# Thresholded attention and a gated feed-forward in one kernel: scores of two key tiles in one run, weight sums in another place, new planner costs and ranks

## The chip, the core and the metric

The kernel runs on one core of one Trainium2 chip. The metric is device time in microseconds for one execution. The kernel before was timed three times: 1387.51, 1389.75 and 1391.09 us, median 1389.75. One further execution was profiled; from its first to its last instruction it spans 1385.8 us, and every duration below is from it. Lower is better.

The engines are called by their short names: PE (TensorE, matrix products), DVE (VectorE), ACT (ScalarE), POOL (GpSimd) and SP (the engine that only issues transfers). PEld is PE's loading of weights, which runs beside its products.

## What is computed

```python
# q, k, v: (8, 8, 576, 64) float32; tau = 0.02
scores = (q @ k^T) / sqrt(64)
thresh = max(scores, over keys) - tau
scores = where(scores >= thresh, scores, -1e9)
attn   = softmax(scores)            # with 1e-9 added to the sum
x      = (attn @ v), heads side by side -> (4608, 512)
h      = x @ w_in                   # (512, 2048)
g      = h / (1 + exp(-1.702 * h))
out    = g @ w_out                  # (2048, 512) -> (4608, 512)
```

All products are done in float32. The two weight matrices arrive as float64 and are converted on the chip.

## The kernel before

**Attention, by pairs.** Two heads of one batch element make a pair; there are 32 pairs, four to a batch element. For each pair n the kernel transposes q and k on DVE (`prep`, L390), so that head h lies on partitions 64h to 64h+63. The 576 keys are four tiles of 128 and a tail of 64. For one key tile t and one half c of the 576 queries, `scores` (matmul at L414) issues two matmuls, one for each head, each on 64 of PE's 128 rows, into one PSUM slot of two banks (pool `psA`, three slots). The tail of both heads together is one product over all 128 rows (L407), with a small block-diagonal weight `kd` that POOL copies (`prep_kd`, L395). ACT copies each slot to SBUF (`keep`, L437). DVE takes the maxima (`in_groups` L451, `over_tiles` L457/L462, `over_groups` L471/L472), lowers them by tau and spreads them over partitions by a trip through DRAM (`lower_rows`, `row_out`, `row_in`) for the first pairs, by `lower` (L477/L482) and `spread_max` (L497) later. `sub` (L523/L528) subtracts; ACT masks and exponentiates (L534, L538). `values` (matmul at L552, 64 columns of PE per head) multiplies with v into a psA slot named `pv`. The sums of the exponentials come from PE for pairs 0 to 4 (`sums_by_pe`) and from DVE later (`in_groups` with add, `one_group` L595). `spread_sums` (L604, L606) inverts and spreads them, and `place_x` (L623) writes the scaled result as the transposed x of the feed-forward's blocks. `place_x` gives the `pv` slot back.

PE thus works in three shapes: 64 rows (scores), 64 columns (values and sums), and the whole array (the tail and the feed-forward).

**Feed-forward, by blocks of 256 tokens.** Blocks 0 and 1 are done plainly and together (`first_blocks`: `mm1_0` L678, `mm2` L660 with 512 columns), while w_in and w_out still arrive and are converted (`cv_ex`, `cv_power`, `cv_frac`, `cv_end`). Blocks 2 to 13 (`feed_forward`) take `mm1` (L638), tanh (L647), `gelu` (L650) and then a second product by seven half-size products instead of eight (`second`, `product`, matmul at L825; the results are gathered by `read`, L847). These need sums of quarters of g, made on POOL after every second gelu (`s_sums`, L791 to L793; `s_last`, L804), and sums of quarters of w_out, made once on POOL in eight operations of 128x1024 (`t_sum`, L785). The last four blocks (`two_blocks`) also use seven products for the first matmul (`product1`, L743); they need `w_sum` (L717) and `x_sum` (L726). Accumulators of the feed-forward lie in pool `psM`, two slots of one bank.

**What sets the order.** Nothing is scheduled at run time. Every piece of work is a `task` with an engine, a cost, a rank, the tasks it follows, and the slots it takes and gives back. `run_in_order` plays these through on a clock: whenever an engine is free it starts the ready task of lowest rank for which the slots are there, and emits its instructions at that moment. The result is a fixed order on each engine; on the chip semaphores keep the true dependencies, and each engine works strictly in its order. Feed-forward products on PE have the rank LAST (1000), and so fill what attention leaves. The tables `EARLY`, `LATER` and `CV` shift ranks by the name of a task. `lag` is the time the planner assumes between the end of a task and its use by another engine (0.06 us unless given). From pair `WHOLE` = 6 on, both halves of a key tile are one task that takes two psA slots (`scores_of`); before that each half is a task of its own.

Of the kernel before, what the change touches and what calls it, by code (L numbers as in the profile page):

```python
# [19 lines left out]
P = 128  # L20
# [10 lines left out]
def kernel(  # L31
# [97 lines left out]
    for x in ("raw0", "raw1", "qkT0", "qkT1", "mb"):  # L129
# [6 lines left out]
        "lower_rows": -1.89,  # L136
        "values": 1.63,
        "exps": 1.38,
        "load_qk": -1.72,
        "prep": -1.69,  # L140
        "load_v": 1.46,
        "mask": 1.64,
        "over_groups": -1.9,
        "sub": -1.05,
        "one_group": 0.95,
        "scores": 0.67,
        "spread_sums": 1.4,
        "sums_by_pe": 2.29,
        "in_groups": 0.61,
        "keep": -1.15,  # L150
    }
    LATER = {
        "in_groups": 0.38,
        "mask": -0.74,
    }
    CV = {
        "cv_power": 0.15,
        "cv_frac": 0.13,
    }

    def task(engine, cost, rank, f, *a, after=(), take=(), give=(), lag=0.06):
        if 0 <= rank < LAST:
            rank += CV.get(f.__name__, 0.0) + (EARLY if a[0] < 2 * NPAIR else LATER).get(f.__name__, 0.0)
        tasks.append((engine, cost, rank, f, a, [x for x in after if x is not None],
                      take, give, lag))
        return len(tasks) - 1
# [3 lines left out]
    def run_in_order():  # L170
# [10 lines left out]
        started = 0  # L181
        while events:
# [18 lines left out]
            for engine, queue in ready.items():  # L201
# [12 lines left out]
                heapq.heappush(events, (now + tasks[i][1], 0, i))  # L214
# [187 lines left out]
    def scores(n, t, c):  # L402
        qT, kT = mats[n, 0], mats[n, 1]
        ps = psA.tile([P, 2, 512], FP32, name="ps", tag="ps")
        if t == NKT:
            for i in range(2):
                nc.tensor.matmul(  # L407
                    ps[:, i, 0:SH], lhsT=kd, rhs=qT[:, ts(i, SH)],
                    start=True, stop=True,
                )  # L410
            del mats[n, 0], mats[n, 1]
        else:
            for h in range(2):
                nc.tensor.matmul(  # L414
                    ps[:, h, 0:SH],
                    lhsT=kT[ts(h, D), ts(t, P)], rhs=qT[ts(h, D), ts(c, SH)],
                    start=True, stop=True,
                )
        pss[n, t, c] = ps

    def scores_of(n, t, cs):
        for c in cs:
            scores(n, t, c)
# [474 lines left out]
    FFU = 1.722  # L898
# [3 lines left out]
    for i in range(len(pieces)):  # L902
# [9 lines left out]
        a = task("POOL", 2.4, rank, load_w, i, after=w_loads[-1:], take=place, lag=5.0)  # L912
        w_loads.append(a)
        e = task("DVE", 0.43, rank, cv_ex, i, after=[a])
        m = task("ACT", 0.79, rank, cv_power, i, after=[e])
        a = task("DVE", 1.14, rank, cv_frac, i, after=[e])

        over = [ready_w[y] for y in range(i) if i >= n_in and stage(y) == (i - n_in) // PER_STAGE]
        ready_w.append(task("DVE", 0.7, rank, cv_end, i, after=[a, m] + over, give=place))
# [8 lines left out]
    def first_blocks():  # L928
        xs = list(placed.values())[-NPAIR:]
        for j in range(NFC):  # L930
# [7 lines left out]
            a = task("ACT", 0.6, FIRST, tanh, j, after=ffn[-1:], take=("io",))  # L938
            gelus[j] = task("DVE", 0.69, FIRST, gelu_0, j, after=[a], give=("psM", "io"))
        for i in range(PLAIN * BLK // P):  # L940
# [7 lines left out]
            a = task("ACT", 0.6, FIRST, half, i, after=ffn[-1:], take=("osb",), give=("psM",))  # L948
            task("SP", 0.6, FIRST, store_0, i, after=[a], give=("osb",), lag=2.2)

        for x in range(4):
            for k in range(2):
                after = t_ready[-1:] + (ffn[-1:] if x > 1 else ffn[2 * NFC : 2 * NFC + 1])
                t_ready.append(
                    task("POOL", 3.0, FIRST, t_sum, x, k, after=after + ready_w[n_in:])
                )

    def feed_forward(blk):
# [3 lines left out]
        for j in range(HF):  # L962
            for f in range(2):
# [6 lines left out]
            a = task("ACT", 0.6, FIRST, tanh, j, after=ffn[-1:], take=("io",))  # L970
            gelus[j] = task(
                "DVE", 0.69, FIRST, gelu, j, after=[a, last_mm2.get(j // 4)],
                give=("psM", "io"),
            )
            if j % 2:
                sums.append(task("POOL", 2.5, FIRST, s_sums, j // 2, after=[gelus[j - 1], gelus[j]]))
        second(blk, 0, {j: [gelus[j]] for j in range(HF)}, sums)

    def second(blk, w, ready, sums):
# [4 lines left out]
        for x, p in order:  # L984
            js = ((0, 4), (4, 8), (4, 7), (7, 8))[p]
            after = ffn[-1:] + t_ready
# [15 lines left out]
            if x == P6:  # L1002
                lasts = [task("POOL", 1.6, FIRST, s_last, k, w, after=ffn[-1:]) for k in range(2)]
            if x == P1:
                a = task("ACT", 0.35, FIRST, read, blk, x, after=ffn[-1:], take=("osb", "osb"))
            else:
                a = task(
                    "DVE", 0.84 if x == P5 else 0.42, FIRST, read, blk, x, after=ffn[-1:] + reads,
# [8 lines left out]
    def two_blocks(blk):  # L1017
# [4 lines left out]
        for x in range(4):  # L1022
            if first:
                done_w.append([task("DVE", 0.66, LAST - 1.0, w_sum, x, 0, nc.vector, after=done_w[-1:][0] if done_w else xs)])
            after = (xd[-1:] or xs) + (done_w[x][:1] if first else []) + last_product1
            xd.append(task("DVE", 0.66, LAST - 1.0, x_sum, blk, x, after=after))
        if first:
            for k in range(1, HF // 2):
                for x in range(4):
                    after = xs + done_w[x - 1][-1:] + done_w[x][-1:]  # L1030
                    done_w[x].append(
                        task("POOL", 1.5, FIRST, w_sum, x, k, nc.gpsimd, after=after)
# [3 lines left out]
        for j in range(HF):  # L1036
            reads = [None] * 7
            for x in range(7):
# [6 lines left out]
                if x == P3:  # L1045
                    after += xs
# [5 lines left out]
                if x == P1:  # L1052
                    a = task("ACT", 0.35, FIRST, read1, j, x, after=ffn[-1:], take=("hs",), give=bank)
                else:
                    a = task(
                        "DVE", 0.84 if x == P5 else 0.42, FIRST, read1, j, x,
# [3 lines left out]
            for h in range(2):  # L1060
                a = task("ACT", 0.6, FIRST, tanh1, j, h, after=[reads[P5 if h == 0 else P3]], take=("io",))
                g1[j, h] = task(
                    "DVE", 0.8, FIRST, gelu1, j, h, after=[a, last_mm2.get(j // 4), g1.get((j, 0))],
                    give=("io", "hs") if h else ("io",),
                )
            if j % 2:
                sums.append(task(
                    "POOL", 2.5, FIRST, s_sums, j // 2, after=[g1[j - 1, 0], g1[j, 0]]
# [5 lines left out]
        a = task("DVE", 1.3, FIRST, s_sum1, 0, after=again + ffn[-3:-2])  # L1074
        b = task("DVE", 1.3, FIRST, s_sum1, 1, after=[a] + ffn[-1:])
        c = task("DVE", 1.3, FIRST, s_sum1, 2, after=[b])
# [7 lines left out]
    for n in range(NP):  # L1084
# [4 lines left out]
        slow = 1.2 if n < NPAIR else 1.0  # L1089
# [4 lines left out]
        lq = task("SP", cost, r - 2.0, load_qk, n, 0, q0, after=behind, take=own(n, "raw0"), lag=2.0)  # L1094
        lk = task(
            "SP", cost if n else 0.1, r - 2.0, load_qk, n, 1, q1, after=behind,
            take=own(n, "raw1"), lag=2.0,
        )
        v_tail = f"v_t{n % 2}"
        lv = task("SP", 2.1, r - 1.2, load_v, n, take=("v_m", v_tail), lag=2.0)  # L1100
        pq = task("DVE", 0.77, r, prep, n, 0, after=[lq], take=own(n, "qkT0"), give=own(n, "raw0"))
        pk = task("DVE", 0.77, r, prep, n, 1, after=[lk], take=own(n, "qkT1"), give=own(n, "raw1"))
        pd = task("POOL", 0.5, r, prep_kd, n, after=[pk], take=("kd",))
# [5 lines left out]
        mx = []  # L1109
        for t in range(NKT + 1):  # L1110
            tail = t == NKT
            copies = []
            if tail or n >= WHOLE:


                cs = range(1 if tail else 2)
                a = task(
                    "PE", (1.2 if tail else 1.35) * slow, r, scores_of, n, t, cs, after=[pq, pk] + ([pd] if tail else []) + after,
                    take=("psA", "s_t") if tail else ("psA", "psA") + own(n, "s_m"),
                    give=own(n, "qkT0", "qkT1") + ("kd",) if tail else (),  # L1120
                )
                after = [a]
                copies = [task("ACT", 0.65, r, keep, n, t, c, after=[a], give=("psA",)) for c in cs]
            else:
                for c in range(2):

                    a = task(
                        "PE", 0.6 * slow, r, scores, n, t, c, after=[pq, pk] + after,
# [105 lines left out]
```

## Time and profile before

| what | before |
|---|---|
| median of three runs | 1389.75 us |
| profiled span | 1385.8 us |
| PE busy | 1330.6 us, 96% |
| DVE busy | 1123.9 us, 81% |
| ACT busy | 639.6 us, 46% |
| POOL busy | 299.8 us, 22% |
| granted PE clock, mean | 0.986 |

How to read it. "Busy" is the union of the records of an engine; matmuls overlap in PE's pipeline, so a mean duration of 382 ns for a 128x256 product does not mean that one starts every 382 ns. The difference of starts in the timeline is the better price. The page also cuts the span into 40 slices of 34.6 us and gives each engine's busy share in tenths; in a group line, "idle before" is the time that an engine stood before such instructions, and the name behind the arrow is what ended most of it. A bracket at the end of a timeline line says the same for that one instruction.

Four groups of PE hold most of its time: the first products of blocks 2 to 13 (L638, 346.3 us), the second products (L825, 205.5 us for the part that reads w_out itself), scores (L414, 162.0 us) and values (L552 into pv, 126.0 us for its largest group). On DVE the transposing reductions (L451) take 315.3 us and the subtraction (L523) 190.6 us.

### The profile page before, as it was taken

How to read it: one execution, taken by the hardware profiler on the slowest of the kernel's cores; microseconds unless marked ns; L12 is line 12 of the kernel's file. 1: busy time of each engine (PE TensorE's matmuls, PEld its weight loads, DVE VectorE, ACT ScalarE, POOL GpSimd, SP SyncE). 2: the span in 40 equal slices, each digit the busy share in tenths (PEclk: the TensorE clock that was granted, in tenths of full speed). 3: DMA queues.
4: the chain of work that ended last, by engine and by line, in shares of the span. 5: the costliest groups of instructions: out<-in, count | busy, mean ns of one | idle time of the engine just before them, and what ended most of it. 6: DMA issues, size and time to landing. Idle time of an engine off the chain costs nothing.

```text
span 1385.8 us, 18139 instructions
## 1 busy us (share of the span) xinstructions
PE 1330.6 (96%) x6792; PEld 1004.2 (72%) x6792; DVE 1123.9 (81%) x1906; ACT 639.6 (46%) x822; POOL 299.8 (22%) x362
## 2 busy tenths in 40 slices
PE   5778999999999999999999999999999999799999
PEld 3446864477777777777777777777777777688887
DVE  7989999978888888889888888888888888762642
ACT  5864663555454545454545445444545454120210
POOL 1121222212131213122212212121212224321120
PEclk9889999999999999999999999999999999999999
DMA  8674973211111111111111011111111100000000
GB/s 173 200 235 132 301 256 67 68 22 22 41 27 41 27 41 21 39 26 34 26 33 35 18 42 26 42 26 42 26 34 25 42 1 8 9 1 16 16 1 31
DMA packets 205379, 78.70 MB, mean 57 GB/s; under 512 B 192747, under 2 KB 192747, under 8 KB 205291
## 3 DMA queue, kind: packets, MB, share of 16 engines
q1 hardware_dynamic: 195723, 43.71, 15.0%
q0 software_dynamic: 7200, 33.55, 7.0%
q8 instruction: 53, 0.87, 0.2%
q10 hardware_dynamic: 2368, 0.30, 0.2%
q14 instruction: 35, 0.29, 0.1%
HBM read 68.05 MB, written 9.47 MB: 56 GB/s over the span
## 4 chain that ended last, share of the span: by engine, by line
PE 84%; DVE 12%; DMA 1%; issue 1%; SPq 1%; ACT 0%; DVEq 0%
PE hps L638 25%; PE ops L825 24%; PE ps L414 9%; PE pv L552 9%; PE ps L743 4%; PE hps L678 4%; PE ps L825 3%; PE ops L743 3%; DVE part L451 3%; PE ps L407 2%; DVE arena L523 2%; SPq L278 1%; PE den L552 1%; DVE red L472 1%; DVE arena L390 1%
## 5 line engine op out<-in xcount | busy, mean ns | idle before, releaser
L451 DVE TRANSPOSE_TENSOR_REDUCE part<-arena 128x36 f32<-128x1152 f32 x236 | 315.3, 1354 | 71.6 <-ACT arena L437 70.9
L638 PE MATMUL hps<-xT,w_in 128*128 128x256 f32 x1536 | 346.3, 382 | 0.0
L638 PEld LDWEIGHTS hps<-xT,w_in 128*128 128x128 f32 x1536 | 287.9, 190 | 56.3 <-issue 18.5
L437 ACT COPY arena<-ps 128x576 f32<-128x576 f32 x288 | 171.1, 641 | 292.3 <-PE ps L414 271.2
L825 PE MATMUL ops<-w_out,arena 128*128 128x256 f32 x896 | 205.5, 382 | 0.0
L534 ACT ACTIVATE arena<-arena 128x1152 f32<-128x1152 f32 (+1 forms) x160 | 168.2, 1060 | 76.3 <-DVE arena L523 70.2
L538 ACT ACTIVATE arena<-arena,shift,scl 128x1152 f32<-128x1152 f32 (+1 forms) x160 | 194.4, 1243 | 1.9
L825 PEld LDWEIGHTS ops<-w_out,arena 128*128 128x128 f32 x896 | 168.0, 190 | 32.8 <-issue 10.0
L523 DVE TENSOR_TENSOR arena<-arena 128x1152 f32<-128x1152 f32 x128 | 190.6, 1528 | 1.3 <-DMA arena<-row 0.6
L414 PE MATMUL ps<-arena 64*128 64x288 f32 x1024 | 162.0, 439 | 21.9 <-DVE arena L390 11.0
L791 POOL TENSOR_TENSOR arena<-arena 128x256 f32<-128x256 f32 x56 | 46.5, 831 | 566.5 <-DVE arena L650 467.4
L414 PEld LDWEIGHTS ps<-arena 64*128 64x128 f32 x1024 | 90.7, 191 | 84.7 <-issue 52.0
L825 PE MATMUL ops<-arena 128*128 128x256 f32 x672 | 149.9, 379 | 0.3 <-DVE osb L847 0.3
L825 PEld LDWEIGHTS ops<-arena 128*128 128x128 f32 x672 | 127.6, 190 | 18.0 <-DVE osb L847 0.7
L552 PE MATMUL pv<-arena 128*64 128x288 f32 x960 | 126.0, 414 | 1.2 <-issue 1.2
L647 ACT ACTIVATE th<-hps 128x512 f32<-128x512 f32 x112 | 66.4, 593 | 127.0 <-PE hps L638 106.0
L552 PEld LDWEIGHTS pv<-arena 128*64 128x64 f32 x960 | 67.0, 138 | 55.7 <-issue 14.6
L390 DVE STREAM_TRANSPOSE arena<-arena 128x576 f32<-128x576 f32 x64 | 48.3, 762 | 37.7 <-PE ps L407 35.3
L804 POOL TENSOR_TENSOR arena<-arena 128x512 f32<-128x512 f32 x28 | 57.5, 2060 | 98.6 <-PE ops L825 98.5
L650 DVE SCALAR_TENSOR_TENSOR arena<-th,hps 128x512 f32<-128x512 f32 x96 | 63.8, 665 | 8.8 <-ACT th L647 8.8
L395 POOL COPY kd<-arena 64x64 f32<-64x64 f32 x64 | 17.6, 275 | 235.0 <-DVE arena L390 191.2
L847 DVE SCALAR_TENSOR_TENSOR osb<-ops,osb 128x256 f32<-128x256 f32 x98 | 38.6, 405 | 34.9 <-PE ops L825 33.2
(122 smaller groups left out, 1422.4 us busy)
## 6 DMA issues: line engine op xcount, KB each, us to landing
arena<-in_q_dram SPq DMA_DIRECT2D x128, 72.0 KB, 2.2
out_dram<-osb SPq DMA_DIRECT2D x36, 256.0 KB, 2.0
arena<-in_k_dram SPq DMA_DIRECT2D x124, 72.0 KB, 2.2
arena<-in_v_dram SPq DMA_DIRECT2D x64, 128.0 KB, 2.4
w_out<-in_moe_w_in_dram POOLq DMA_DIRECT2D x12, 512.0 KB, 5.8
arena<-in_moe_w_out_dram POOLq DMA_DIRECT2D x12, 512.0 KB, 5.4
w_out<-in_moe_w_in_dram POOLq DMA_DIRECT2D x12, 511.6 KB, 7.0
arena<-in_moe_w_out_dram POOLq DMA_DIRECT2D x12, 511.6 KB, 6.3
```

Source lines behind the costliest of these rows:

```text
L414: nc.tensor.matmul(ps[:, h, 0:SH], lhsT=kT[ts(h, D), ts(t, P)], rhs=qT[ts(h, D), ts(c, SH)], start=True, stop=True,)
L437: nc.scalar.copy(out=o, in_=pss.pop((n, t, c))[:, :, 0:SH])
L451: nc.vector.tensor_reduce(out=o, in_=i, axis=AXL.X, op=op, apply_transpose=True)
L523: nc.vector.tensor_tensor(out=s, in0=s, in1=mb, op=ALU.subtract)
L534: nc.scalar.activation(out=s, in_=s, func=AF.Prelu, alpha=STEEP)
L538: nc.scalar.activation(out=s, in_=s, func=AF.Exp, scale=scl, bias=shift)
L552: nc.tensor.matmul(o[c][ts(h, D), 0:SH], lhsT=lhsT, rhs=rhs, start=(t == 0), stop=(t == NKT),)
L638: nc.tensor.matmul(hidden[j][:, ts(f, BLK)], lhsT=w_in[:, c, ds((f * HF + j) * P, P)], rhs=xTs[blk][:, c, :], start=(c == 0), stop=(c == N ...
L647: nc.scalar.activation(out=ths[j], in_=hidden[j], func=AF.Tanh, scale=GELU_SCALE / 2)
L650: nc.vector.scalar_tensor_tensor(out=g[:, :, j, :], in0=two(ths.pop(j)), scalar=1.0, in1=two(hidden.pop(j)), op0=ALU.add, op1=ALU.mult,)
L743: nc.tensor.matmul(places[j, x], lhsT=left[:, c, ts(j, P)], rhs=right[:, c, :], start=(c == 0), stop=(c == 1),)
L825: nc.tensor.matmul(banks[blk][k][:, ts(o, HM)], lhsT=left[:, j, :], rhs=right[:, j, :], start=(j == 0), stop=(j == HF - 1),)
```

## The change

1. From pair 6 on, two key tiles' scores are one task, `scores_two`: eight matmul instructions in one run. The 576 queries are split 320/256 instead of 288/288. The first 320 queries of each tile go to a slot of their own (`near`), the last 256 of both tiles share a third one (`far`), so a run takes all three psA slots. `keep_two` copies 640 or 512 elements a partition instead of 576. The tail has a task of its own, `tail_scores`.
2. `t_sum` is no longer issued by `first_blocks`. Its eight operations are issued in `feed_forward` of block 2, after the first gelu sums (`j == 1`), one behind the other. Each product waits in the planner only for the sums that it reads (`T_OF`).
3. `tau_terms` comes after the two transposes of pair 0 in the planner.
4. In `two_blocks`, the planner lets all first products of the first two blocks follow every pair's `place_x`, not only the last kind.
5. The planner knows a cost for changing PE's shape (`MODES`, `ENTER`), has lags by engine (`LAG`), and other costs and lags for nearly every task. The rank tables are all new.

```diff
     EARLY = {
-        "lower_rows": -1.89,
-        "values": 1.63,
...
+        "exps": -1.33,
+        "in_groups": 1.05,
...
     LATER = {
-        "in_groups": 0.38,
-        "mask": -0.74,
+        "exps": -1.22,
+        "in_groups": 5.45,
...
     CV = {
-        "cv_power": 0.15,
-        "cv_frac": 0.13,
+        "cv_end": -6.59,
...
+    LAG = {"PE": 0.26, "DVE": 0.18, "ACT": 0.22, "POOL": 0.18}
+    MODES = {
+        "scores": 0, "scores_two": 0, "values": 1, "sums_by_pe": 1, "tail_scores": 2, "product": 2,
+        "product1": 2, "mm1": 2, "mm1_0": 2, "mm2": 2,
+    }
+    ENTER = (0.2, 0.1, 0.1)
...
-                heapq.heappush(events, (now + tasks[i][1], 0, i))
+                cost = tasks[i][1]
+                if engine == "PE":
+                    last, mode = mode, MODES[tasks[i][3].__name__]
+                    cost += ENTER[mode] if mode != last else 0.0
+                heapq.heappush(events, (now + cost, 0, i))
...
+    FAR = S - BLK
+
+    def scores_two(n, t):
+        near = [psA.tile([P, 2, 512], FP32, name="ps", tag="ps") for _ in range(2)]
+        far = psA.tile([P, 2, 512], FP32, name="ps", tag="ps")
+        for u, part in ((0, 0), (0, 1), (1, 1), (1, 0)):
+            qs = ds(FAR, BLK) if part else ds(0, FAR)
+            for h in range(2):
+                o = far[:, h, ts(u, BLK)] if part else near[u][:, h, 0:FAR]
                 nc.tensor.matmul(
+                    o, lhsT=mats[n, 1][ts(h, D), ts(t + u, P)], rhs=mats[n, 0][ts(h, D), qs],
                     start=True, stop=True,
                 )
+        for u in range(2):
+            pss[n, t + u, 0], pss[n, t + u, 1] = near[u][:, :, 0:FAR], far[:, :, ts(u, BLK)]
+
+    def keep_two(n, t, c):
+        if c == 0:
+            sT[n, t] = seat_scores(n, t).rearrange("p (h s) -> p h s", h=2)
+        o = sT[n, t][:, :, ds(FAR, BLK)] if c else sT[n, t][:, :, 0:FAR]
+        nc.scalar.copy(out=o, in_=pss.pop((n, t, c)))
...
-        for x in range(4):
-            for k in range(2):
-                after = t_ready[-1:] + (ffn[-1:] if x > 1 else ffn[2 * NFC : 2 * NFC + 1])
-                t_ready.append(
-                    task("POOL", 3.0, FIRST, t_sum, x, k, after=after + ready_w[n_in:])
-                )
...
+            if j == 1 and blk == PLAIN:
+                for y in range(8):
+                    after = t_ready[-1:] + sums[-1:] + ready_w[n_in:]
+                    t_ready.append(task("POOL", 2.4, FIRST, t_sum, *divmod(y, 2), after=after))
...
+    T_OF = {P6: 4, P7: 8, P4: 6, P5: 2}
...
-            after = ffn[-1:] + t_ready
+            after = ffn[-1:]
+            if x in T_OF:
+                after += t_ready[: T_OF[x]]
...
-                if x == P3:
+                if x == P3 or first:
                     after += xs
...
+        if n == 0:
+            tasks[tau_done][5].extend([pq, pk])
...
-            if tail or n >= WHOLE:
-                cs = range(1 if tail else 2)
                 a = task(
-                    "PE", (1.2 if tail else 1.35) * slow, r, scores_of, n, t, cs, after=[pq, pk] + ([pd] if tail else []) + after,
-                    take=("psA", "s_t") if tail else ("psA", "psA") + own(n, "s_m"),
...
+            if n >= WHOLE and not tail:
+                if t % 2 == 0:
+                    a = task(
+                        "PE", 1.94, r, scores_two, n, t, after=[pq, pk] + after,
+                        take=("psA",) * 3 + ("s_m",) * 2,
+                    )
+                    after = [a]
+                b = task("ACT", 0.6, r, keep_two, n, t, 0, after=[a], give=("psA",))
+                c = task(
+                    "ACT", 0.48, r, keep_two, n, t, 1, after=[a, b] + far, give=("psA",) * (t % 2)
+                )
...
-            a = task("ACT", 0.6, FIRST, tanh, j, after=ffn[-1:], take=("io",))
+            a = task("ACT", 0.48, FIRST, tanh, j, after=ffn[-1:], take=("io",))
...
-                "DVE", (0.76 if n in BY_DMA else 1.5) if tail else 1.36, r, sub, n, t, after=subs[-1:],
+                "DVE", (0.67 if n in BY_DMA else 1.55) if tail else 1.35, r, sub, n, t, after=subs[-1:],
```

## The prediction

> **What bounds the kernel now.** I read the page's slices first, then a table by stage, then TensorE's timeline inside the longest stage, then the waits.
>
> ```profile
> PE   5778999999999999999999999999999999799999
> DVE  7989999978888888889888888888888888762642
> PEclk9889999999999999999999999999999999999999
> ...
> 122.00:284.00 162.00, 152.84 (x673) 94.84 (x672) 152.03 (x247) 81.74 (x100) 37.67 (x46) 0.98 0.52 153
> 284.00:1175.00 891.00, 890.68 (x4673) 686.09 (x4673) 761.58 (x1270) 445.19 (x561) 195.71 (x218) 1.00 0.14 30
> 1175.00:1193.00 18.00, 10.52 (x42) 7.83 (x39) 15.13 (x23) 0.37 (x1) 11.43 (x9) 0.81 0.04 15
> ```
>
> Stage columns are length, then busy PE, PEld, DVE, ACT, POOL. From 284 to 1175 us TensorE is busy 890.68 of 891 us, VectorE 761.58 (85%). There only a shorter PE programme shortens the kernel. "Busy" hides something, though:
>
> ```profile
> 609.80 1.24 PE L414 MATMUL ps<-arena 64*128 64x288 f32 x8
> 610.98 1.99 PE L638 MATMUL hps<-xT,w_in 128*128 128x256 f32 x8
> 612.90 4.10 PE L552 MATMUL pv<-arena 128*64 128x288 f32 x32
> 616.83 1.14 PE L552 MATMUL pv<-arena,v_t 128*64 128x288 f32 x8
> 617.90 1.24 PE L414 MATMUL ps<-arena 64*128 64x288 f32 x8
> ...
> 364.93 20.88 PE L638 MATMUL hps<-xT,w_in 128*128 128x256 f32 x96
> 385.74 1.24 PE L414 MATMUL ps<-arena 64*128 64x288 f32 x8
> ```
>
> Each matmul instruction leaves two records. Start to start, 96 full-array records take 20.81 us, 0.216 each; eight of them between two score tiles take 612.90-610.98 = 1.92 instead of 1.73. Single records show where it goes. Going from full-array to 64-row scores, the first gap is 0.309 instead of 0.216 and the next 0.340 instead of 0.236: 0.197 us for one switch. Scores to full array: (0.332-0.236)+(0.320-0.216) = 0.20; into 64-column values 0.144; values to scores or to full array 0.20.
>
> Two places where PE does wait:
>
> ```profile
> 268.07 4.69 POOL L785 TENSOR_TENSOR arena<-w_out,arena 128x1024 f32<-128x1024 f32 x2
> 272.72 4.63 POOL L785 TENSOR_TENSOR w_out<-w_out 128x1024 f32<-128x1024 f32 x2
> 268.27 2.23 DVE L472 TENSOR_TENSOR red<-red,fold 64x36 f32<-64x36 f32 x1
> 270.54 2.26 DVE L471 COPY fold<-red 32x36 f32<-32x36 f32 x1
> 272.83 2.27 DVE L472 TENSOR_TENSOR red<-red,fold 32x36 f32<-32x36 f32 x1
> 275.14 2.79 DVE L595 TENSOR_SCALAR r<-red 32x18 f32<-32x18 f32 x4
> 280.24 2.29 PE L414 MATMUL ps<-arena 64*128 64x288 f32 x8 [6.45 <-DVE xT L623]
> ...
> 1187.28 2.04 PE L743 MATMUL ps<-arena 128*128 128x256 f32 x4 [6.28 <-DVE arena L726]
> 1192.23 1.10 PE L743 MATMUL ps<-arena,w_in 128*128 128x256 f32 x4 [1.21 <-DVE arena L726]
> ```
>
> First: while GpSimd runs the weight sums (t_sum), tiny VectorE operations of 0.18 us take 2.2 us, the place_x behind them is late, and PE waits 6.45 us for its PSUM slot. Second: after the last pair's values PE has only 3.5 us of products left, then waits for the sums of x. After both, the stage table asked for 276.80-283.50 and 1184.80-1191.40 gives a PE clock of 0.50.
>
> **What the Trainium skill says.** "TensorEngine Tiling (Array Packing)", Key Properties: "Changing tiling mode (not just tile) drains the TensorE". The trace agrees, 0.14 to 0.20 us a switch. "SBUF — State Buffer", Who interferes with whom: a VectorE instruction with two SBUF inputs, or a copy or tensor_scalar in a two-port mode, is blocked for a whole GpSimd instruction that reads SBUF; a tensor_reduce never is. The trace agrees: 2.2 us each above, one POOL operation being 2.34; the part reductions at 213.72 keep their 1.3 us under the same sums. "TensorE: Matmul & The Clock Gate", What's actually happening: after about 3.4 us idle the array clock halves until it has been busy as long; the two half-clock windows here follow the two waits of over 6 us.
>
> **The change part by part.** The instruction order of the changed kernel on each engine is known; durations are from the profile of before.
>
> (1) Scores in runs of eight. Columns stay the same: per two tiles four row pairs of 320 and four of 256 for eight of 288. Pairs start 0.2425 apart at 288; with 0.2158 at 256 columns I interpolate 0.269 at 320, so 4x0.269+4x0.216 = 1.94 = 8x0.2425. ACT's copies: 640+512 elements for 576+576, nothing. What falls is switches. From the first feed-forward matmul on, the order of before has 80 into scores, 104 out of them, 28 into values, 24 values-to-scores, 4 values-to-full; after: 52, 52, 28, 0, 28. Priced as above: 46.4 against 30.4 us, -16.0, all on the path since PE is full. Bounds -14 to -17. ACT, POOL and the DMA queues only change order here.
>
> (2) The last pair. After its values the new order has 48 product instructions (96 records, 20.7 us) where before had 8. In before, the last x sum released PE 1192.2-1175.6 = 16.7 us after the values; in the new VectorE order w_sum and x_sum still follow place_x at once. So 6.28+1.21 waited and half of the 3.75 us run at half clock go: -9.4. Bounds 0 to -9.4.
>
> (3) t_sum leaves the first blocks: 6.45, 1.6 at 211.8 (a matmul waiting for w_out's conversion, 2.06 for 0.43), 1.3 at 221 and half of 3.26 at half clock: -11.0. PE's work from first to last instruction of those blocks is then continuous by my walk: values of pair 6 at about 240, their exponentials ready near 234; two-tile scores behind them at about 250, pair 6's place_x near 246. Bounds -5 to -11.
>
> (4) Start. q and k of pair 0 are issued by 2.8 and 2.9 us and land 2.2 later (page's DMA list); before, their transposes sat behind tau's terms until 6.86. Moved ahead they can start at 5.1. VectorE's work up to the fourth pair's place_x is 102.4 us for 103.5. That puts the first feed-forward matmul, which now comes before the last scores of pair 5 (1.7 us), at 117.1 for 122.2: -5.1+1.7 = -3.4. Bounds 0 to -6, since DMA waits of 2.9 us near 100 could move.
>
> (5) t_sum behind the third block's first gelu sums: eight GpSimd operations of 2.34 us in a row, 18.7 us. Queued on POOL behind them are the block's other gelu sums (wanted some 30 us later) and a kd copy: harmless. VectorE is not. Call the end of that block's second gelu 0 (about 288 us). The first gelu sums end at 2.9, t_sum runs to 21.6. VectorE then has the third gelu, a part_t, three part reductions (done near 8), and then six small blockable operations (two of L462, four of L471/L472) at one POOL operation each: until 21.8 instead of 9.2. Reciprocal-side scalars 0.7, two transposes 1.35, then gelu four at 24.5. PE needs that gelu's PSUM slot after 24 instructions (10.4 us), values of pair 8 (5.2), a tail (1.0) and 12 instructions, near 15: it waits 9.5, then 1.6 more at half clock: +11.1. Below: 0 if VectorE meets the window in reductions and transposes, which are not blocked. Above: the whole window, +18. I take +11.
>
> (6) A two-tile run takes all three psA slots, so it cannot start until pv's slot is given back by place_x; before, scores took two and often stood directly behind the values. VectorE needs about 4.4 us for it (0.79 over tiles, 0.86 folds, 0.71 sums, 1.05 reciprocal and spread, 0.95 place). The new order puts at least 16 full instructions (6.9 us) between values and scores in the steady part, but VectorE is at 85%, 87% with PE faster, and the planner's sub costs 1.35 where the trace has 1.53. I take +3, bounds 0 to +20; it names psA and nothing else queued behind.
>
> Planner costs, lags, xs on the first product1 and the per-product t_ready only choose the order; no instruction is added: 0.
>
> Sum: -16.0-9.4-11.0-3.4+11.1+3 = -25.7. Against the profiled span of 1385.8: 1360.1. The median of runs stands 3.95 above that span, so 1364.
>
> **Rivals.** A, as summed: 1364, own range 1356 to 1373. B, t_sum's block is hidden because VectorE falls elsewhere in its row: 1364-11 = 1353. For it: only some operations are blockable; against: six stand in line. C, scores wait for place_x half a us in each of 24 pairs and the tail's wait half remains: 1364-3+12+5 = 1378. D, slower: the same slot, priced higher. If place_x stands behind one train of part reductions (5.1 us) in every pair, it needs 9.5 us where 6.9 to 7.9 are given: 2 us of idle PE in 24 pairs, 1364-3+48 = 1409. It decides from (25.7+3)/24 = 1.2 us a pair. Against it: that train is short of the 13% of VectorE time that is free. That the switches don't shrink is excluded; the order is fixed.
>
> **How the numbers follow.** A 0.50, B 0.22, C 0.17, D 0.07, and 0.04 for no visible change, within 0.3% of 1389.75 (4.2 us), which is about what a measurement tells from none. Faster 0.89, same 0.04, slower 0.07. The range takes A and B whole and most of C: 1349 to 1381.
>
> **What would show it.** Score groups of 16 records lasting some 2.1 us start to start, and a PE programme 16 us shorter between equal work; no wait on L801's sums; t_sum around 290-310 with 2.2 us VectorE dwarfs beside it and a PE wait near 303 on a gelu. Wrong if scores show PE waits on place_x in every pair, or if PE before 120 us is later than now.

## The result, and the profile after

| | before | after |
|---|---|---|
| median of four runs each, side by side | 1390.42 us | 1372.78 us (1371.34 to 1373.55) |
| ratio | | 0.9878, 95% interval 0.9863 to 0.9894 |
| profiled span | 1385.8 us | 1369.5 us |
| PE busy | 1330.6 us | 1315.9 us |
| DVE busy | 1123.9 us | 1111.1 us |
| mean granted PE clock | 0.986 | 0.986 |

The change makes the kernel 1.2% faster. The forecast was 1364, range 1349 to 1381.

In the changed kernel's source all line numbers have moved: two-tile scores are L487, single-tile scores L462, values L627, `mm1` L713, `gelu` L725, `product` L900, `product1` L818, `read` L922, `t_sum` L860, `s_sums` L866 to L868, `sub` L598 and L603, and the folds of `over_groups` L546 and L547. First its slices, and the same stages as before, cut at 1165 because the last pair now ends there:

```profile
PE   5769999988999999999999999999999999999999
PEclk9998999998999999999999999999999999999999
...
284.00:1165.00 881.00, 865.32 (x4585) 680.24 (x4583) 759.25 (x1260) 433.95 (x547) 196.97 (x224) 0.99 0.14 29
1165.00:1176.00 11.00, 10.43 (x48) 9.22 (x49) 2.97 (x8) 0.37 (x1) 10.84 (x9) 1.00 0.13 49
```

Before's PE row had a 7 six slices from the right; here there is a 9. Its slices nine and ten (274 to 342 us), 9 before, are 8 now, and in the tenth the clock row has an 8. The two stage lines give the length and then the busy time of PE: it is idle 881.00-865.32 = 15.7 us in the long stage, where before it was idle 0.3. The largest piece of it stands here, in the timelines of PE, POOL and DVE:

```profile
297.89 5.34 PE L713 MATMUL hps<-xT,w_in 128*128 128x256 f32 x24
312.06 3.75 PE L713 MATMUL hps<-xT,w_in 128*128 128x256 f32 x8 [8.83 <-DVE arena L725]
...
295.31 9.28 POOL L860 TENSOR_TENSOR arena<-w_out,arena 128x1024 f32<-128x1024 f32 x4
304.54 4.64 POOL L860 TENSOR_TENSOR w_out<-w_out 128x1024 f32<-128x1024 f32 x2
...
304.67 2.25 DVE L546 COPY fold<-red 32x36 f32<-32x36 f32 x1
306.95 2.27 DVE L547 TENSOR_TENSOR red<-red,fold 32x36 f32<-32x36 f32 x1
311.36 0.65 DVE L725 SCALAR_TENSOR_TENSOR arena<-th,hps 128x512 f32<-128x512 f32 x1
```

The bracket of the second line says that PE stood 8.83 us for a gelu (L725). Below it is why: while POOL runs the weight sums, a fold that takes 0.18 us elsewhere takes 2.25, and the gelu is queued behind six such operations. The rest is scattered. One of these small waits:

```profile
392.87 3.89 DVE L526 TRANSPOSE_TENSOR_REDUCE part<-arena 128x36 f32<-128x1152 f32 x3
396.69 0.65 DVE L725 SCALAR_TENSOR_TENSOR arena<-th,hps 128x512 f32<-128x512 f32 x1
...
385.98 10.74 PE L713 MATMUL hps<-xT,w_in 128*128 128x256 f32 x48
397.39 1.99 PE L713 MATMUL hps<-xT,w_in 128*128 128x256 f32 x8 [0.67 <-DVE arena L725]
```

The gelu starts only when three part reductions are through (392.87 to 396.7), and PE starts 0.7 us after it. No such wait stands before a score. Three, of 0.6 us in all, are for a psA slot: values that wait for a score copy (L498) to give theirs back.

**A ledger.** From the first feed-forward matmul to the last one, every gap between the starts of two matmul records is split into its steady pitch (0.216 us for 256 columns and so on), a price for each change of shape (those of the prediction), and what is left, which is waiting and half clock. The shape column is therefore a count times a price; what tests the prices is that nothing is left over where PE does not wait. All in us:

| kernel | first feed-forward matmul at | steady work | shape changes | left to 285 | 285-350 | 350-1140 | after 1140 |
|---|---|---|---|---|---|---|---|
| before | 122.2 | 1192.1 | 46.4 | 10.9 | 0.0 | 0.1 | 10.4 |
| after | 118.8 | 1194.5 | 30.8 | 0.2 | 11.7 | 8.6 | 1.2 |

The sum of the differences is -3.4+2.4-15.6-10.7+11.7+8.5-9.2 = -16.3, and the spans differ by 1385.8-1369.5 = 16.3.

### The profile page after: what moved, and what is told of

It reads as the page before. It is cut to its first block, busy times and chain, and to the rows that moved or that the text cites. A ratio compares the mean times of both kernels' runs of the same rounds, so it can differ in the third digit from the quotient of the medians.

```text
span 1369.5 us, 18133 instructions
## 1 busy us (share of the span) xinstructions
PE 1315.9 (96%) x6792; PEld 1010.6 (74%) x6792; DVE 1111.1 (81%) x1906; ACT 638.0 (47%) x822; POOL 279.9 (20%) x362
## 4 chain that ended last, share of the span: by engine, by line
PE 64%; DVE 23%; ACT 8%; issue 3%; DMA 1%; SPq 1%; DVEq 0%; ACTq 0%
PE ops L900 20%; PE hps L713 13%; PE pv L627 9%; PE ps L487 5%; DVE part L526 5%; PE ps L818 4%; DVE arena L598 4%; PE ps L900 4%; PE ops L735 3%; ACT arena L613 3%; ACT arena L609 3%; PE ops L818 3%; DVE arena L725 2%; PE ps L472 2%; DVE arena L572 1%
## 5 line engine op out<-in xcount | busy, mean ns | idle before, releaser
L713 PE MATMUL hps<-xT,w_in 128*128 128x256 f32 x1536 | 343.2, 382 | 10.9 <-DVE arena L725 10.9
L713 PEld LDWEIGHTS hps<-xT,w_in 128*128 128x128 f32 x1536 | 290.8, 191 | 61.4 <-DVE arena L725 14.3
L526 DVE TRANSPOSE_TENSOR_REDUCE part<-arena 128x36 f32<-128x1152 f32 x236 | 310.6, 1349 | 25.9 <-ACT arena L498 24.2
L900 PE MATMUL ops<-w_out,arena 128*128 128x256 f32 x896 | 206.4, 382 | 2.9 <-DVE arena L725 2.9
L613 ACT ACTIVATE arena<-arena,shift,scl 128x1152 f32<-128x1152 f32 (+1 forms) x160 | 200.0, 1250 | 4.5
L900 PEld LDWEIGHTS ops<-w_out,arena 128*128 128x128 f32 x896 | 168.1, 190 | 36.5 <-issue 8.3
L598 DVE TENSOR_TENSOR arena<-arena 128x1152 f32<-128x1152 f32 x128 | 175.5, 1417 | 0.6
L498 ACT COPY arena<-ps 128x640 f32<-128x640 f32 x208 | 122.4, 643 | 105.0 <-PE ps L487 104.7
L866 POOL TENSOR_TENSOR arena<-arena 128x256 f32<-128x256 f32 x56 | 51.9, 927 | 501.9 <-DVE arena L725 392.5
L900 PE MATMUL ops<-arena 128*128 128x256 f32 x672 | 152.7, 381 | 1.8 <-DVE osb L922 1.8
L900 PEld LDWEIGHTS ops<-arena 128*128 128x128 f32 x672 | 126.7, 190 | 24.0 <-issue 3.1
L627 PE MATMUL pv<-arena 128*64 128x288 f32 x960 | 124.8, 411 | 0.6 <-ACT arena L498 0.6
L487 PE MATMUL ps<-arena 64*128 64x320 f32 (+1 forms) x832 | 115.0, 416 | 0.0
L512 ACT COPY arena<-ps 128x576 f32<-128x576 f32 x80 | 49.0, 643 | 134.8 <-PE ps L472 114.7
L627 PEld LDWEIGHTS pv<-arena 128*64 128x64 f32 x960 | 66.9, 137 | 53.8 <-ACT arena L498 5.9
L725 DVE SCALAR_TENSOR_TENSOR arena<-th,hps 128x512 f32<-128x512 f32 x96 | 64.3, 670 | 48.6 <-ACT th L722 47.7
L487 PEld LDWEIGHTS ps<-arena 64*128 64x128 f32 x832 | 76.1, 186 | 32.1 <-issue 16.8
L922 DVE SCALAR_TENSOR_TENSOR osb<-ops,osb 128x256 f32<-128x256 f32 x98 | 39.0, 409 | 64.0 <-PE ops L900 59.5
L452 POOL COPY kd<-arena 64x64 f32<-64x64 f32 x64 | 15.6, 244 | 332.0 <-DVE arena L447 298.9
L447 DVE STREAM_TRANSPOSE arena<-arena 128x576 f32<-128x576 f32 x64 | 46.3, 754 | 16.3 <-PE ps L472 7.9
```

The lines of the kernel that those rows point to most:

```text
L487: nc.tensor.matmul(o, lhsT=mats[n, 1][ts(h, D), ts(t + u, P)], rhs=mats[n, 0][ts(h, D), qs], start=True, stop=True,)
L498: nc.scalar.copy(out=o, in_=pss.pop((n, t, c)))
L526: nc.vector.tensor_reduce(out=o, in_=i, axis=AXL.X, op=op, apply_transpose=True)
L598: nc.vector.tensor_tensor(out=s, in0=s, in1=mb, op=ALU.subtract)
L613: nc.scalar.activation(out=s, in_=s, func=AF.Exp, scale=scl, bias=shift)
L627: nc.tensor.matmul(o[c][ts(h, D), 0:SH], lhsT=lhsT, rhs=rhs, start=(t == 0), stop=(t == NKT),)
```

## The experiments

My theory was the ledger: shape changes, the end and the early weight sums gave what was forecast, the moved weight sums took back 11.7, and small gelu waits took 8.5 that had not been forecast in that size. The rivals: that the small waits come from the three PSUM slots of a two-tile run; that the weight sums cost by their total time and not by being in line with small operations; that ranks and costs and not the score run made the gain. Ratios are to the kernel before, timed beside each, with 95% intervals; the kernel after stands at 0.9878.

**e1: each weight sum in four pieces.**

```diff
-        o, a, b = (y[:, ts(k, 4), :] for y in T_SUMS[x])
-        nc.gpsimd.tensor_tensor(out=o, in0=a, in1=b, op=ALU.subtract)
+        for i in range(k * 4, (k + 1) * 4):
+            o, a, b = (y[:, ts(i, 1), :] for y in T_SUMS[x])
+            nc.gpsimd.tensor_tensor(out=o, in0=a, in1=b, op=ALU.subtract)
```

> The changed kernel with each of the eight weight sums of 128x1024 elements issued as four GpSimd operations of 128x256; the order on every engine is otherwise the same. My theory: the PE wait of 8.8 us at 303 is six small VectorE operations in a row, each of which loses one whole GpSimd operation (2.2 us). With pieces of some 0.7 us each of the six should take about 0.7, the gelu behind them should be done near 302, and PE should wait 1 us or less there and stay at full clock: about 10 us below the changed kernel, 1361 to 1364. Rival 1, that the total time GpSimd is on the shared port decides: pieces have an overhead each, the window grows from 18.7 to some 25 us, and the wait stays or grows: 1372 to 1378. Rival 2, that the gelu waits for something else (its tanh, its PSUM slot): 1373, unchanged.

Measured: 1372.05 us (1371.12 to 1377.03), ratio 0.9883 (0.9864 to 0.9902): no gain. The profiled execution is the 1377.03 one. Its timeline, DVE, POOL and PE:

```profile
297.95 16.16 DVE L537 TENSOR_TENSOR red<-red,part_t 64x18 f32<-64x18 f32 x2
...
297.49 10.97 POOL L861 TENSOR_TENSOR arena<-w_out,arena 128x256 f32<-128x256 f32 x16
...
317.81 2.50 PE L713 MATMUL hps<-xT,w_in 128*128 128x256 f32 x5 [13.26 <-DVE arena L725]
```

The first of these two small sums has a record of 15.98 us, the second 0.17. It did not lose one GpSimd operation; it stood for 23 of them (one every 0.685 us) until the train ended at 313.9. Then everything behind it ran at full speed. PE waited 13.26 us.

**e2: in two pieces** (128x512, the same edit with `ts(i, 2)`).

> As the quarters, but each weight sum is two GpSimd operations of 128x512 (some 1.25 us). My theory, one GpSimd operation lost by each blocked VectorE operation: six operations take 1.2 us instead of 2.25, so the gelu comes 6 us earlier, the wait at 303 shrinks from 8.8 to 2.5 to 3.5 us and the half clock behind it goes: 6 to 7.5 us below the changed kernel, 1365 to 1367. Rival (GpSimd's total time decides): 1372 to 1376, the wait 9 us.

Measured: 1371.17 us (1369.84 to 1372.02), ratio 0.987 (0.9852 to 0.9887).

```profile
302.22 1.20 DVE L547 TENSOR_TENSOR red<-red,fold 32x36 f32<-32x36 f32 x1
303.46 4.83 DVE L670 TENSOR_SCALAR r<-red 32x18 f32<-32x18 f32 x4
...
310.38 3.78 PE L713 MATMUL hps<-xT,w_in 128*128 128x256 f32 x8 [6.78 <-DVE arena L725]
```

Here the rule holds: each blocked operation loses one GpSimd operation, 1.20 us where one comes every 1.23. But the wait is 6.78, not 3. The four scalar operations (L670) behind the folds, which took 0.17 each in the changed kernel because the train was over by then, now come inside it and take 1.21 each. A shorter piece frees the operations in line sooner, and the next ones in line meet the rest of the train.

**e12: the quarters, profiled again.**

> The same kernel as e1, profiled a second time. In e1 the profiled execution took 1377.0 us and the other four 1371.1 to 1372.3. If VectorE is starved by every train of short GpSimd operations, the second of the two small sums at 298 again takes some 16 us and PE waits some 13 us for the gelu. If the starvation is a matter of timing between the two engines, the operations take 0.65 to a few us each here, the wait is 6 to 9 us, and the span is near 1370.

Measured: 1371.15 us. This time the sum that starved in e1 took 0.30 us and the nine operations behind it 0.63 to 0.67 each; PE waited 1.95 us for that gelu. Then another small sum stood 4.65 us, seven pieces, and two later gelus cost 2.0 and 2.5. The ledger has 10.1 us left between 285 and 350, against 11.7 after and 16.2 in e1. So the theory of one operation lost by each blocked one holds in most places; the starvation is real but not the same in every execution; and the split gained next to nothing in sum: a train of 20 us of back-to-back sums meets whatever VectorE has next in line.

**e5: the sums spread, two behind each of the block's four gelu sums.**

```diff
-            if j == 1 and blk == PLAIN:
-                for y in range(8):
+            if j % 2 and blk == PLAIN:
+                for y in range(j - 1, j + 1):
```

> The changed kernel with the eight weight sums spread over the third block: two behind each of its four gelu sums instead of eight behind the first. What the quarters and halves showed: a blocked VectorE operation loses one GpSimd operation (1.20 us of 1.23, 2.27 of 2.32) or, if the operations come every 0.68 us, the whole train (16.0 us); so a delay is bounded by the length of a train. Trains of 4.7 us then delay a gelu by at most 4.7 us, and PE's slack in front of the gelu at 303 was about 13.2-8.8 = 4.4 us: the wait of 8.8 us and the half clock behind it go, 9 to 11 us below the changed kernel, 1361 to 1365, and no wait above 1.5 us between 290 and 340. Rival, that the port's total time counts: four windows each cost 2 to 3 us, 1369 to 1373. Rival on the other side: products wait for the sums, which now end late in the block, 1374 and more.

Measured: 1366.22 us (1364.97 to 1366.3), ratio 0.9824 (0.981 to 0.9839). The ledger has 4.0 us left in 285 to 350 for 11.7; the largest wait there, in PE's timeline, is

```profile
323.21 3.29 PE L900 MATMUL ops<-w_out,arena 128*128 128x256 f32 x14 [2.37 <-DVE arena L725]
```

The wait at 303 is gone, and the largest that is left is shorter than one train of two sums (4.7 us). The expected bound of 1.5 us for it was too low.

**e6: the sums on VectorE, one behind each gelu of that block.**

```diff
+            if blk == PLAIN:
+                after = t_ready[-1:] + [gelus[j]] + ready_w[n_in:]
+                t_ready.append(task("DVE", 1.14, FIRST, t_sum, *divmod(j, 2), after=after))
...
-        nc.gpsimd.tensor_tensor(out=o, in0=a, in1=b, op=ALU.subtract)
+        nc.vector.tensor_tensor(out=o, in0=a, in1=b, op=ALU.subtract)
```

> The changed kernel with the eight weight sums as VectorE operations, one behind each gelu of the third block, none on GpSimd. VectorE's sums of the same shape take 1.14 us (s_sum1), so 9.1 us of its own work replace 18.7 us of a shared port. My theory: no operation is blocked, so six times 2.1 us go and 9.1 us come, spread over some 40 us in which VectorE has 13% free; the wait at 303 becomes several of under 2 us: 6 to 10 us below the changed kernel, 1363 to 1367. Rival: VectorE is full there, so its 9.1 us are all paid: 1371 to 1374.

Measured: 1368.69 us (1367.71 to 1369.19), ratio 0.9843 (0.9829 to 0.9858). Nothing is left in 285 to 350. But 350 to 1140 has 12.2 for 8.6, and the end 4.2 for 1.2: PE waits 2.18 us there for a read of an accumulator (L922) that stands on DVE behind sums of w_in and x, and then runs at half clock for 3.4 us. This order has 44 product instructions behind the last values instead of 48, so PE comes to that read 1.7 us sooner; that this is the whole reason is not shown. Each sum takes DVE 1.21 us where GpSimd needs 2.35.

**e3: the sums back in the first blocks** (the loop of the old `first_blocks`, at the new cost; the one behind the gelu sums removed).

> The changed kernel with the weight sums issued in the first two blocks again, as in the kernel before; the planner makes the order anew. My ledger: the move saved 10.9 us in the first blocks and cost 11.7 behind the third block's gelu sums, so it was worth nothing: 1371 to 1374, with PE waits of 6 us near 270 and none of 9 near 303. Rival: the move itself was a gain (the early waits would be larger in the new order, since more score work hangs on VectorE there): 1376 to 1384. Rival on the other side: 1362 to 1368, if the new order meets the early window with operations that are not blocked.

Measured: 1377.83 us (1377.35 to 1379.87), ratio 0.9921 (0.9906 to 0.9936): 5 us above after, so the first rival here was right. PE's two waits:

```profile
217.99 2.08 PE L735 MATMUL ops<-w_out,arena 128*128 128x512 f32 x2 [4.43 <-DVE w_out L436]
300.30 8.04 PE L713 MATMUL hps<-xT,w_in 128*128 128x256 f32 x23 [6.09 <-DVE arena L725]
```

The sums hold up a conversion of w_out at 212 and stretch a pair's threshold at 282. The ledger has 7.3 + 10.3 left up to 350, after 0.2 + 11.7.

**e4: one key tile per task again**, halves of 288 and two slots, all else as changed.

```diff
-                if t % 2 == 0:
-                    a = task(
-                        "PE", 1.94, r, scores_two, n, t, after=[pq, pk] + after,
-                        take=("psA",) * 3 + ("s_m",) * 2,
-                    )
...
+                a = task(
+                    "PE", 0.97, r, scores_of, n, t, after=[pq, pk] + after,
+                    take=("psA", "psA", "s_m"),
+                )
```

> The changed kernel with one key tile's scores per planner task again, in halves of 288 columns and two PSUM slots; the rest (ranks, costs, weight sums' place, tau) as changed. PE's order then has 243 tile shape switches from the first feed-forward matmul on for 160, priced at 47.0 us for 30.4. My theory, that the switches are what the two-tile run saves: 16 us more, 1386 to 1391, with steady waits like those of the changed kernel (some 9 us). Rival 1: the steady waits of 9 us come from the three PSUM slots, so that they vanish here: 1377 to 1381. Rival 2: the new order's packing matters more than its switches: 1372 to 1377.

Measured: 1394.99 us (1393.87 to 1395.86), ratio 1.0043 (1.0028 to 1.0058), 22.2 above after and some 4 above what was expected. The ledger: shape changes 47.4 for 30.8, which is 16.6; the weight sums' window 18.8 for 11.7, since they now catch a threshold in front of a score:

```profile
318.48 2.29 PE L462 MATMUL ps<-arena 64*128 64x288 f32 x8 [15.85 <-DVE thr L556]
```

The small waits from 350 to 1140 are 6.5 for 8.6, so without three slots at once most of their sum is still there. They are not quite the same waits: PE's list for that stretch has 2.5 us for gelus, where the changed kernel has 4.3, and 1.7 us for place_x.

**e8: one planner cost.**

```diff
-                "DVE", (0.67 if n in BY_DMA else 1.55) if tail else 1.35, r, sub, n, t, after=subs[-1:],
+                "DVE", (0.67 if n in BY_DMA else 1.55) if tail else 1.53 if 8 < n < 28 else 1.35, r, sub, n, t, after=subs[-1:],
```

> The changed kernel with one planner cost changed: the subtraction of the row maximum is 1.53 us for pairs 9 to 27, as the trace has it with GpSimd and VectorE both running, instead of 1.35; shape switches and the work behind the last values stay at the same counts. My theory: the 9 us of waits of 0.5 to 1.2 us each after 370 are gelus and reads that the planner thought done, because VectorE's train in front of them is longer than it was told: they fall to 4 us or less, 1367 to 1369. Rival 1, that the waits come from GpSimd's gelu sums blocking subtractions in an order that the planner can't see: another order has as many of them, 1371 to 1374. Rival 2, packing gets worse: 1375 and more.

Measured: 1365.41 us (1364.82 to 1367.34), ratio 0.9823 (0.9808 to 0.9838), better than expected. From PE's waits:

```profile
PE hps L713 <- DVE arena L725: 8.9, 1, 8.9
PE ops L900 <- DVE osb L922: 1.2, 2, 0.9
PE ops L900 <- DVE arena L725: 0.8, 1, 0.8
```

The columns are total, times and longest: gelus held up PE's first and second products once each, where in the changed kernel it was five times (10.9 us) and four times (2.9 us). What is left from 350 to 1140 falls from 8.6 to 2.5. The cost of 1.53 was the mean in the kernel before; in the changed one the subtraction takes 1.45 us on average after 360 (median 1.35; 11 of 84 are held up beyond 1.6 us). So the edit gives the planner a little more than the truth. That an order made with this margin has fewer small waits is shown, and it came back in both other orders that had it (e10 below has 5.1 us where e6, without it, has 12.2); whether long trains or held-up subtractions make a gelu late without it, the runs do not tell apart.

**e7 and e11: the two-tile run alone, on the kernel before.** `scores_two` and `keep_two` as in the change, old ranks and costs. In e7 two products of the last blocks stood ahead of three pairs' scores, in memory that those pairs still needed, so its last blocks are computed from other data; e11 holds these products back:

```diff
-                if x == P3:
+                if x == P3 or first:
                     after += xs
```

> The kernel before with the two-tile score run alone; ranks, costs, weight sums' place and tau as before. PE's order then has 149 shape switches from the first feed-forward matmul on, 28.3 us by the same prices for 46.4: 18 us less. But its order leaves 12 product instructions (5.2 us) less behind the last pair's values than before. My theory: 18 us less and 5 more at the end, the weight sums' waits as before: 1376 to 1380. Rival 1, three slots taken at once make scores wait for place_x when the planner doesn't price it: 1384 to 1395, with waits on L623 in many pairs. Rival 2, the ranks and costs do most of the work: within 3 us of before.

> The kernel before with the two-tile score run alone, as e7, with one line more: the products of the last two blocks wait until the last pair is placed. In e7, without it, the first two of these products stood ahead of three pairs' scores and used memory that those pairs still needed. The order still runs out of feed-forward work early: behind the values of the pair before the last two there are only 2 full instructions until the last values. My theory, that the old ranks and costs let the scores of the last pairs fall behind: three bare chains of some 18 us each stay, 1430 to 1450, although the shape switches cost 28.3 us for 46.4. Rival, that the misplaced products held TensorE up: 1376 to 1385.

Measured: e7 1448.3 us (ratio 1.0419, 1.0402 to 1.0436), e11 1448.93 us (ratio 1.0427, 1.041 to 1.0445). My expectation for e7 missed by 70 us; that for e11 held. PE's timeline in e11:

```profile
1197.33 4.21 PE L434 MATMUL ps<-arena 64*128 64x320 f32 x16 [15.41 <-DVE arena L390]
...
1222.35 2.19 PE L574 MATMUL pv<-arena 128*64 128x288 f32 x8 [9.83 <-ACT arena L560]
...
1246.81 2.05 PE L765 MATMUL ps<-arena 128*128 128x256 f32 x4 [10.74 <-DVE arena L748]
```

PE waits for a transpose of q or k, for exponentials and for sums of x, and has nothing to do beside: the feed-forward was used up, and three pairs were still to be done. The ledger has shape changes of 28.3, as counted, but some 52 us left between 1175 and 1250, and 15.4 between 576 and 596 where a transpose came late. Here the score run paid only in an order that keeps feed-forward work for the last pairs. Whether the ranks, the costs or the lags of the change give that order was not taken apart. Neither part alone beats the kernel before: all of the change but the score run is 0.4% slower than it (e4, where 7.1 us are the larger weight-sum window), the score run under the old plan 4.3% slower (e11), and the two together are 1.2% faster.

**e9 and e10: the edits together.** e9 is e5 with e8's cost, e10 is e6 with it.

> The changed kernel with both edits that helped: the weight sums spread two behind each of the third block's four gelu sums, and the planner's subtraction at 1.53 us for pairs 9 to 27. The first took 7.8 us of waits near 303, the second 6.8 us of small waits after 370, at different places. My theory: they add, some 7 us of waits are left of 21.7 after the first feed-forward matmul, 1357 to 1361. Rival: both only move VectorE's load, so what one saves comes back with the other: 1364 to 1367.

> The changed kernel with the weight sums on VectorE, one behind each gelu of the third block, and the planner's subtraction at 1.53 us for pairs 9 to 27; 48 product instructions stand behind the last values again, where the version with VectorE alone had 44 and lost 4.1 us there. My theory: 6 to 8 us of waits are left, 1358 to 1362, the same as spread GpSimd sums, since neither blocks. Rival: VectorE's 9.1 us more of work stay visible in the next blocks (1.1 us each at 350, 375, 450, 475), 1363 to 1367.

Measured: e9 1361.3 us (1360.39 to 1362.56), ratio 0.9795 (0.9781 to 0.981); e10 1357.38 us (1355.64 to 1358.76), ratio 0.9766 (0.9751 to 0.978). e10 beats both kernels: 15.4 us below after. Its ledger has 0.0 left in 285 to 350, 5.1 from 350 to 1140 and 1.2 at the end. In e10 the gains more than add: 4.1 us (e6) and 7.4 us (e8) by themselves, 15.4 together, because the 12.2 and 4.2 us that e6 had from 350 on are 5.1 and 1.2 here. In e9 they add less than in full, 6.6 and 7.4 apart and 11.5 together: PE still waits 4.5 us for one gelu from 319 on, so spread GpSimd sums depend on what VectorE happens to have in line.

## Why the prediction was right, point by point

- **Step 1, shape changes, -16.0: right.** 46.4 to 30.8 in the ledger, -15.6. The prices hold: with them before has 0.1 us left in 790 us of its steady part. (They are rounded: with 0.197 for a change into scores, as the step has it, its own counts give 46.2 and 30.3.) Undone in e4, the same term is +16.6.
- **Step 2, the end, -9.4: right.** 10.4 to 1.2. No wait on the sums of x remains; 48 product instructions cover them, and 0.9 us for a read behind them is what is left. With 44 (e6) 3 us come back through that read, and with four (e11) the sums of x alone cost 10.7. This term is owed to the new order, not to the score run: e4 has the new plan without the run, and no more left at the end than the changed kernel.
- **Step 3, early weight sums, -11.0, and step 5, the moved ones, +11.1: right in place and size.** 10.9 to 0.2, and 0.0 to 11.7. The forecast had a wait of 9.5 us near 303 on gelu four behind six blocked operations; it is 8.83 us, at 303, behind those six. That the two cancel is so only against the old order: in the new one, putting the sums back (e3) costs 5 us.
- **Step 4, the start, -3.4: failed.** The mis-sized term is the landing of q and k, 1.5 us of the 2.4 that are missing. I had assumed that both transposes could start at 5.1, 2.2 us after the issue. DVE now waits for q until 6.63:

```profile
6.63 1.44 DVE L447 STREAM_TRANSPOSE arena<-arena 128x576 f32<-128x576 f32 x2 [6.63 <-DMA arena<-in_q_dram]
```

  tau's terms had been hidden behind that transfer. The 2.2 us was the median of all transfers of q and of the later ones of k; the DMA list of before gives the first four of k, which ACT issues, a line of their own with 3.3. In the changed kernel and in the ten experiments that have this start, the first scores start between 8.12 and 8.45 us; before they started at 8.35. The work that moved behind the first feed-forward matmul is 2.4 us, not 1.7; with the first matmul 3.4 us earlier that leaves -1.0. The step's own parts (1.76 at the start, 1.1 of VectorE's work, 1.7 of scores that go behind) make 4.6 and not 5.1; where the rest comes from it doesn't say. In those ten that matmul comes between 119.1 and 121.4, so even this is at the good end.
- **Step 6, +3 for scores waiting on place_x: failed in mechanism, and 5.5 us short.** PE's waits name place_x in front of scores for 0.4 us in all, once, for a single-tile score, and a psA slot in front of values for 0.6. What came is 8.5 us, mostly gelus and reads that DVE reached half a us to one us late. The step mentioned the subtraction's cost but tied it to psA alone. The new order puts feed-forward products closer to their gelus than DVE can follow; e8 shows what a wider cost is worth. What brought the order there is open: from 350 to 1140 PE's waits for gelus are 4.3 us in the changed kernel, 2.5 with the new costs and the old score tasks (e4), 1.4 with the old costs and the new score run (e11) and none before.

The misses, 2.4 for the start and 5.5 for the small waits, with 0.4 + 0.2 + 0.3 + 0.6 of small ones in steps 1, 2, 3 and 5, are the 9.4 us by which the sum of -25.7 missed -16.3. (The medians stand 8.8 apart, since the median lies 3.3 us above the profiled span after and not 3.95.) Both large misses went the same way, and they used up rival A's own range of 1356 to 1373; the stated range held with room because it took in rival C, whose mechanism did not occur. Of the rivals, B (the moved sums hidden) did not come about by itself, but e6 and e10 reach it by moving the sums to DVE. C and D, scores waiting for place_x pair after pair, did not occur.

## What to carry to other kernels

A term of a plan that is hidden today (tau's terms behind a transfer, a gelu behind a full PE) has no price until the trace shows what it is hidden behind: look for the releaser, then ask what comes second. A planner's costs are also its margins: with the new plan eight waits of 0.5 to 1.1 us stood in 790 us where the old plan had none, and raising one cost by 0.18 us, a little above the truth, left two of them. Long back-to-back GpSimd work beside small VectorE operations was best given to VectorE here, or spread out; cutting it into smaller pieces left the train as long as it was. And two changes that each lose alone can win together, so a part of a plan is tested inside the plan it was made for.

## What the runs showed of the hardware

- "SBUF — State Buffer", Who interferes with whom, of the Trainium skill has the blocked engine stand for the whole instruction of the other. With GpSimd operations of 2.35 and 1.27 us that is what the traces show: 2.27 and 1.20 us each. With operations of 0.73 us, one every 0.685, it is only sometimes so: 0.63 to 0.67 us in one execution, but one VectorE operation of 0.17 us stood 15.98 us (23 operations) in another, and one 4.65 us (seven) later in the first. Why the waiting operation misses so many turns with short ones, the runs don't tell.
- A subtraction of 128x1024 takes 2.35 us on GpSimd and 1.21 us on VectorE.
- In eleven profiles of orders with the changed start, the first feed-forward matmul, 120 us in, came between 118.8 and 121.4 us, a spread of 2.6 where the start's edit gained 1.0.
- PE's half clock does not need the 3.4 us of idle time that the prediction cites. In each trace the half-clock stretches after 125 us lie on a fixed grid of 3.41 us. In e12 a wait of 1.95 us inside one step of the grid (PE busy 1.46 of 3.41 us from 303.62) brought 3.41 us of half clock; a wait of 2.47 us in the same execution, spread over two steps (busy 1.63 and 2.72 from 324.10), brought none. Over all the traces full clock fell to half after every step in which PE was busy 46% or less, and after none with 48% or more.
